# Batch 0 of a fused attention and feed-forward kernel: two pairs' kv in one PSUM bank, an earlier table load, late x blocks side by side

## The chip, the cores and the metric

One core of one Trainium2 chip. The metric is the device time of one execution in microseconds, as the median of several runs. Kernels are compared only within the same rounds. "Ratio" is always the mean time of one kernel's fast runs over that of the other's fast runs of the same rounds, so it is not quite the ratio of the medians that are quoted. A profiled span is some 1.9 us shorter than the device time of the same execution (284.4 against 286.36 for the kernel before). The experiments ran in three groups on three chips, so times are compared within a group only, and profiles by the distance between two events of one trace: the second profiles, x2 first and no late x on one; kv later and x3 on VectorE on another; the parts alone and v first on the third.

## The reference

```python
# q, k, v: 8 batches x 8 heads x 576 x 64, fp32
q_s = softmax(q, axis=head_dim)                 # per row
k_s = softmax(k, axis=sequence)                 # per column
kv  = einsum('bhsd,bhse->bhde', k_s, v)         # 64 x 64 per head
x   = einsum('bhsd,bhde->bhse', q_s, kv)        # then heads side by side: 4608 x 512
out = gelu_exact(x @ w_in) @ w_out              # w_in 512 x 2048, w_out 2048 x 512
```

## The kernel before

Everything is bf16 on TensorE with fp32 sums in PSUM. A batch goes through these stages: exp of q and k on ScalarE; normalisation and transposition of q (`qT`); `kv` of two heads at a time (a "pair", four per batch), divided by the column sums of exp(k); `x` of each pair, one 128x512 matmul, copied to SBUF as block 0 to 3 of `xT`; then h (16 tiles of 4 matmuls, one for each x block), Gelu, y. TensorE should never stand still, so each batch's attention is worked into the y matmuls of the batch before. Batch 0 has no such cover: its attention is the start of the kernel, while the weights are still arriving.

```python
def kv_pair(b, hp):                       # kv of one pair, in a bank of its own
    ps = psum_a.tile([128, 512], FP32, tag="a")
    for n in range(NS):
        nc.tensor.matmul(ps[:, 0:D + 1], ek_pair[hp // 2][:, hp % 2, n, :],
                         v_pair[b][:, hp, n, 0:D + 1], start=(n == 0), stop=(n == NS - 1))

def norm_pair(b, hp, eng1):               # column D holds the sums
    nc.vector.reciprocal(rec[:, 0:1], ps[:, D:D + 1])
    for hh in range(2):                   # second half on ScalarE if eng1 == "s"
        ...   # kvbd[...] = ps[pr, 0:D] * rec[pr, 0:1]

def x_step(b, hp, eng="v"):               # one matmul, one copy (VectorE, or ScalarE if "s")
    x_mm(b, hp); x_evac(b, hp, eng)

# batch 0 (... = cuts)
kv_pair(0, 0); tp_mm(0, 1)
norm_pair(0, 0, "v")
tp_evac(0, 1, "s")                        # second half of qT, on ScalarE
kv_pair(0, 1); norm_pair(0, 1, "v")
x_step(0, 0)
kv_pair(0, 2); kv_pair(0, 3)
x_step(0, 1, "s")
norm_pair(0, 2, "s"); norm_pair(0, 3, "s")
table(AF.Gelu)                            # a one-element Gelu, to load its table
h_phase(0, {...}, groups={0: 2},          # first two h tiles together, block by block
        pre={1: [lambda: x_step(0, 2)],   # before block 1
             2: [lambda: x_step(0, 3)]})  # before block 2
...
# batch 1, worked into the end of batch 0's y
tp_step(1, 0); tp_step(1, 1)              # after y tiles 0 to 11
...                                       # y tiles 12, 13
kv_pair(1, 0); norm_pair(1, 0, "s")       # first use of batch 1's v
y_end(0); y_end(1)                        # y tiles 14, 15 of two column blocks
...
# transfers, in the order of issue, all from one queue
# q0 k0 v0 | w_in in 5 blocks | w_out blocks 0-2 | q1 k1 | w_out block 3 (2 halves) | v1 (4 pairs) | ...
```

The softmax here doesn't subtract the row's maximum and nothing guards it: scores larger than these inputs give would overflow.

## Time and profile before

| | before |
|---|---|
| device time, median of the first 3 runs | 286.33 us (286.24 to 286.64) |
| profiled span | 284.4 us |
| TensorE busy | 97% |
| "steady h": first h tiles at full speed (weights of their last x block, block 3, loaded) | 17.68 us |
| first y matmul | 30.19 us |
| batch 1's first kv matmul | 43.17 us |
| start of the last copy of output | 281.03 us |

How to read it: the engines run beside each other, and TensorE is the one that is nearly always busy. So time can only be won where TensorE stands still. The table's middle rows are mile posts of TensorE. The prediction below shows the lines of the chain. In the profile's lines PE is TensorE, PEld its weight loads, DVE VectorE, ACT ScalarE, POOL GpSimd, and SPq and ACTq the sequencers that issue transfers; a line gives start, length, engine and what was done, and in brackets how long the engine had been idle and what ended that.

### The profile page before, as it was taken

To read this page: it belongs to the slowest core of one execution; us is meant where nothing else is said; L and a number is where in the kernel's file an instruction comes from. 1 tells how busy PE (TensorE), PEld (TensorE's weight loads), DVE (VectorE), ACT (ScalarE), POOL (GpSimd) and SP (SyncE) were. 2 spreads that over 40 slices of the span, in tenths; PEclk is the share of its full clock that TensorE was granted. 3 is DMA by queue.
4 is the path that set the end of the run, shared out by engine and by line. 5 is a ranking of instruction groups with operands and counts; after the bars stand their busy time and mean duration, and the time that the engine had idled before them with its cause. 6 is when DMAs were issued, how large, how long until landed. Compare 5 with 4: busy or idle time off the path is not lost.

```text
span 284.4 us, 3842 instructions
## 1 busy us (share of the span) xinstructions
PE 276.6 (97%) x1484; PEld 131.1 (46%) x1511; DVE 119.4 (42%) x239; ACT 159.7 (56%) x266; POOL 38.6 (14%) x34
## 2 busy tenths in 40 slices
PE   8989999999999999999999999999999999999995
PEld 3534455445445445444544454445444444444443
DVE  7664388028696454354434532453225111110012
ACT  4876595779565934694368526872576165017400
POOL 5830033002020050005000500040001300000000
PEclk9999999999999999999999999999999999999999
DMA  7999999999529939922993199517500600120033
GB/s 239 378 383 387 372 388 309 308 298 233 143 62 268 297 92 246 248 96 88 233 271 102 74 212 277 140 74 170 127 0 37 184 2 0 74 76 0 0 74 76
DMA packets 58593, 50.05 MB, mean 176 GB/s; under 512 B 26704, under 2 KB 48464, under 8 KB 58576
## 3 DMA queue, kind: packets, MB, share of 16 engines
q1 hardware_dynamic: 58288, 49.68, 61.1%
q8 instruction: 12, 0.20, 0.3%
q10 hardware_dynamic: 288, 0.13, 0.2%
q14 instruction: 5, 0.04, 0.1%
HBM read 36.70 MB, written 9.44 MB: 162 GB/s over the span
## 4 chain that ended last, share of the span: by engine, by line
PE 91%; DMA 3%; DVE 2%; ACT 2%; issue 1%; DVEq 0%; ACTq 0%
PE ps L376 40%; PE ps L386 40%; PE ps L476 3%; DMA f<-in_k_dram 3%; PE ps L251 2%; PE ps L408 1%; PE ps L346 1%; PE ps L323 1%; DVE xT L356 1%; ACT ek L145 1%; DVE kvbd L212 1%; PE ps L197 1%; PE ps L255 0%; PE ps L288 0%; ACT L145 0%
## 5 line engine op out<-in xcount | busy, mean ns | idle before, releaser
L381 ACT ACTIVATE g<-ps 128x512 bf16<-128x512 f32 x144 | 85.7, 597 | 93.4 <-PE ps L376 93.4
L376 PE MATMUL ps<-xT,wi_bf 128*128 128x512 bf16 x560 | 128.6, 379 | 1.3 <-DVE xT L356 0.3
L386 PE MATMUL ps<-wo_bf,g 128*128 128x512 bf16 x549 | 123.2, 379 | 0.6
L376 PEld LDWEIGHTS <-wi_bf 128*128 128x128 bf16 x576 | 55.3, 98 | 66.0 <-issue 2.8
L386 PEld LDWEIGHTS <-g 128*128 128x128 bf16 x560 | 54.6, 98 | 64.9
L393 DVE COPY y_sb<-ps 128x512 f32<-128x512 f32 x35 | 23.9, 686 | 74.9 <-PE ps L386 74.6
L243 POOL TENSOR_TENSOR e<-e,recq 128x1024 bf16<-128x1024 bf16 (+1 forms) x10 | 27.6, 2761 | 178.8 <-ACT ek L148 95.7
L356 DVE CAST xT<-ps 128x512 bf16<-128x512 f32 x32 | 20.6, 686 | 32.6 <-PE ps L346 22.5
L241 DVE TENSOR_REDUCE qsum<-e 128x16 f32<-128x1024 bf16 (+1 forms) x13 | 21.1, 1624 | 8.4 <-ACT e L145 7.0
L224 DVE CAST v_aug<-f 128x512 bf16<-128x512 f32 x24 | 10.3, 429 | 10.0 <-DMA f<-in_v_dram 9.3
L148 ACT ACTIVATE e<-f 128x512 bf16<-128x512 f32 (+2 forms) x28 | 13.2, 540 | 0.1
L97 ACT ACT_TABLE_LOAD x9 | 11.5, 1283 | 2.8 <-issue 2.6
L273 DVE TENSOR_SCALAR kvbd<-ps,rec 64x64 bf16<-64x64 f32 x48 | 11.6, 280 | 0.8
L476 PE MATMUL ps<-kvbd 128*128 128x512 bf16 x35 | 10.3, 462 | 1.2 <-DVE scr L85 1.2
L148 ACT ACTIVATE ek<-f 128x512 bf16<-128x512 f32 x20 | 10.9, 613 | 0.0
L182 ACT ACTIVATE ek<-f 64x1152 bf16<-64x1152 f32 x8 | 9.3, 1162 | 1.7 <-DMA f<-in_k_dram 1.5
L145 ACT ACTIVATE e<-f 128x1024 bf16<-128x1024 f32 (+1 forms) x7 | 6.8, 990 | 3.2 <-DMA f<-in_q_dram 3.2
L251 PEld LDWEIGHTS <-ek 128*128 128x128 bf16 x96 | 6.8, 97 | 3.2 <-ACT ek L145 0.6
L251 PE MATMUL ps<-v_aug,ek 128*128 128x129 bf16 x96 | 8.1, 220 | 0.1
L467 DVE CAST wo_bf<-w 128x2048 bf16<-128x2048 f32 (+1 forms) x5 | 5.1, 1014 | 5.8 <-DMA w<-in_moe_w_out_dram 5.7
L476 PEld LDWEIGHTS <-kvbd 128*128 128x128 bf16 x35 | 3.9, 116 | 6.6 <-issue 3.2
L216 DVE CAST vr_aug<-f 64x512 bf16<-64x512 f32 x6 | 2.5, 416 | 8.7 <-DMA f<-in_v_dram 8.7
(52 smaller groups left out, 98.6 us busy)
## 6 DMA issues: line engine op xcount, KB each, us to landing
out_dram<-y_sb SPq DMA_DIRECT2D x32, 256.0 KB, 2.4
f<-in_q_dram SPq DMA_DIRECT2D x6, 1024.0 KB, 7.7
f<-in_k_dram SPq DMA_DIRECT2D x6, 1024.0 KB, 10.8
f<-in_v_dram SPq DMA_DIRECT2D x6, 1024.0 KB, 9.6
w<-in_moe_w_in_dram SPq DMA_DIRECT2D x6, 512.0 KB, 8.6
w<-in_moe_w_out_dram SPq DMA_DIRECT2D x3, 1024.0 KB, 12.8
f<-in_k_dram SPq DMA_DIRECT2D x4, 576.0 KB, 8.6
f<-in_v_dram SPq DMA_DIRECT2D x8, 288.0 KB, 8.1
```

The source lines that it names most:

```text
L97: nc.scalar.activation(out=scr[:, 1:2], in_=scr[:, 0:1], func=func)
L148: nc.scalar.activation(out=dst[:, s::4], in_=src[:, u::4], func=AF.Exp)
L241: nc.vector.reduce_sum(out=qsum, in_=eq[:, :, hs, :], axis=AX.X)
L243: eng.tensor_tensor(out=eq[:, :, hs, :], in0=eq[:, :, hs, :], in1=recq.unsqueeze(3).to_broadcast([128, J, w, D]), op=ALU.mult,)
L251: nc.tensor.matmul(ps, st[b]["ek"][:, j, hs, :].rearrange("p h d -> p (h d)"), v_aug[b % 2][:, j, hp, 0:PW], start=(j == 0), stop=False,)
L273: nc.vector.tensor_scalar_mul(out=kvbd[b][pr, hps[i], c * 64:c * 64 + 64], in0=ps[pr, i, c * (D + 1):c * (D + 1) + D], scalar1=rec[pr, i:i ...
L356: nc.vector.tensor_copy(out=st[b]["xT"][:, hp, :], in_=ps)
L376: nc.tensor.matmul(ps, wi_bf[:, dm, t * 128:(t + 1) * 128], xT[:, dm, :], start=(dm == 0), stop=(dm == NDM - 1),)
L381: nc.scalar.activation(out=g[:, t, :], in_=ps, func=AF.Gelu)
L386: nc.tensor.matmul(ps, st[c]["g"][:, t, j * 128:(j + 1) * 128], wo_bf[:, t, :], start=(t == 0), stop=(t == NDF - 1),)
L393: nc.vector.tensor_copy(out=y_sb, in_=ps)
L476: nc.tensor.matmul(ps, zeros[:, 0:128], zeros, start=True, stop=True)
```

## The change

The intent is to shorten the stretch from 12 to 18 us. Pairs 2 and 3 share a PSUM bank, so that one reciprocal and two multiplies (with the reciprocal broadcast along the row) serve both. The Gelu table is loaded right after the exps. ScalarE copies x0 and x1, VectorE copies qT. x2 and x3 are both multiplied ahead of the second x block of h, and copied by two engines side by side.

```diff
+    def kv_two(b):
+        ps = psum_a.tile([128, 2, 256], FP32, tag="a")
+        ...                            # pair 2+i in ps[:, i, :], one pair after the other
+    def norm_two(b):
+        nc.vector.reciprocal(rec, ps[:, :, D])
+        for hh in range(2):
+            pr = slice(hh * 64, hh * 64 + 64)
+            nc.vector.tensor_tensor(out=kvbd[b][pr, 2:4, ...], in0=ps[pr, :, 0:D],
+                in1=rec[pr].unsqueeze(2).to_broadcast([64, 2, D]), op=ALU.mult)
@@ batch 0 @@
     tp_mm(0, 1)
+    table(AF.Gelu)
     norm_pair(0, 0, "v")
-    tp_evac(0, 1, "s")
     kv_pair(0, 1)
     norm_pair(0, 1, "v")
-    x_step(0, 0)
-    kv_pair(0, 2)
-    kv_pair(0, 3)
+    x_step(0, 0, "s")
+    tp_evac(0, 1)
+    kv_two(0)
     x_step(0, 1, "s")
-    norm_pair(0, 2, "s")
-    norm_pair(0, 3, "s")
-    table(AF.Gelu)
+    norm_two(0)
     h_phase(0, {...}, groups={0: 2}, pre={
-        1: [lambda: x_step(0, 2)],
-        2: [lambda: x_step(0, 3)],
+        1: [lambda: x_step(0, 2), lambda: x_step(0, 3, "s")],
     })
```

More of the change, by code (lines that the diff above doesn't have):

```diff
@@ L212, in norm_pair @@
                 nc.vector.tensor_scalar_mul(out=dst, in0=ps[pr, 0:D], scalar1=rec[pr, 0:1])
+    def kv_two(b):
+        ps = psum_a.tile([128, 2, 256], FP32, tag="a")
+        st[b]["kvt"] = ps
+        for i in range(2):
+            for n in range(NS):
+                nc.tensor.matmul(
+                    ps[:, i, 0:D + 1], ek_pair[1][:, i, n, :], v_pair[b][:, 2 + i, n, 0:D + 1],
+                    start=(n == 0), stop=(n == NS - 1),
+                )
+    def norm_two(b):
+        ps = st[b]["kvt"]
+        rec = small.tile([128, 2], FP32, tag="reck")
+        nc.vector.reciprocal(rec, ps[:, :, D])
+        for hh in range(2):
+            pr = slice(hh * 64, hh * 64 + 64)
+            nc.vector.tensor_tensor(
+                out=kvbd[b][pr, 2:4, hh * 64:hh * 64 + 64], in0=ps[pr, :, 0:D],
+                in1=rec[pr].unsqueeze(2).to_broadcast([64, 2, D]), op=ALU.mult,
+            )
     def cast_vr(b):
```

## The prediction

> **What bounds the kernel now.** I read the page first: shares of the engines and the chain that ended last.
>
> ```profile
> PE 276.6 (97%) x1484; PEld 131.1 (46%) x1511; DVE 119.4 (42%) x239; ACT 159.7 (56%) x266; POOL 38.6 (14%) x34
> PE 91%; DMA 3%; DVE 2%; ACT 2%; issue 1%; DVEq 0%; ACTq 0%
> ```
>
> TensorE is busy 97% of 284.4 us and carries 91% of the chain. A change that leaves the matmuls alone can win only where TensorE waits. The change touches batch 0's attention step, so next I asked for the chain of waits from 10 to 19 us:
>
> ```profile
> 14.00 0.29 DVE kvbd L212
> 14.29 0.03 issue
> 14.32 0.69 DVE xT L356
> 15.01 0.08 DVE rec L205
> ...
> 15.12 0.28 DVE kvbd L212
> 15.39 0.09 DVE rec L205
> 15.48 0.01 issue
> 15.49 0.32 ACT kvbd L210
> 15.81 0.05 issue
> 15.86 0.40 PE ps L323
> 16.26 0.02 issue
> 16.28 1.35 DVE xT L356 x2
> 17.63 0.04 issue
> 17.68 1.46 PE ps L376 x6
> ```
>
> Columns are start, length, what. Between 12.6 and 17.6 us VectorE sets the pace: copy of x0, normalisation of pair 2 (its second half on ScalarE), the x2 matmul, then two x copies one after the other. Only at 17.68 does TensorE begin the last input block of the first two h tiles; from there it runs without a gap (11.95 us busy of the stretch 18 to 30). This 5 us is all that the change can shorten.
>
> Then I asked where a shift of TensorE would meet something that does not shift. The stretches of busy time and the timelines of GpSimd and TensorE around batch 1's first kv say:
>
> ```profile
> 30.00:45.00 15.00, 14.95 (x96) 7.66 (x97) 10.68 (x15) 10.56 (x12) 4.50 (x5) 1.00 1.07 376
> 42.13 1.42 POOL L188 CAST v_aug<-f 128x576 bf16<-128x576 f32 x2 [3.35 <-DMA f<-in_v_dram]
> 41.45 1.89 PE L386 MATMUL ps<-wo_bf,g 128*128 128x512 bf16 x8
> 43.17 0.45 PE L197 MATMUL ps<-v_aug,ek 128*128 128x65 bf16 x9
> ```
>
> In the first line the last two figures are the DMA share (1.07, so full) and 376 GB/s. GpSimd sat idle 3.35 us for batch 1's v and cast its first pair from 42.13; that cast lasts 0.67 us (664 to 669 ns), so it is done at 42.80. The kv matmul that needs it started at 43.17. Batch 1's v is held by a full DMA, not by compute; TensorE is some 0.3 us behind it.
>
> **What the Trainium skill says.** (1) "VectorE: DVE Perf Modes", section on the TRN2 errata, gives an fp32 tensor_tensor as (N+151)/0.96 ns. For N=128 that is 291 ns (estimate from that page). The trace has no such shape, but its 128x1024 tensor_tensor took 1225 ns at best against 1224 by the formula, and its PSUM copy of 128 columns 292 ns. (2) "SBUF — State Buffer", Who interferes with whom, says that a VectorE instruction with at most one SBUF input outside the 2-port modes does not contend with GpSimd. The new multiplies read PSUM and one SBUF operand, so GpSimd's weight casts at 14.26 to 16.9 us should not stretch them. The trace shows the other side only: tensor_tensor with two SBUF inputs took 1600 ns at 38.26 us, where GpSimd was still busy until 38.78, against 1225 alone. (3) "ScalarE: Activation LUTs", What ACT_TABLE_LOAD costs: about 1283 ns for the load plus a 1380 ns drain. The trace agrees on the load (mean 1283 ns) but not on a drain here: load at 16.14, next activation at 17.44. (4) "PSUM — Partial Sum Buffer", The four PSUM rules: two accumulation groups open at once in one bank must not both clear it. Here pair 2's nine matmuls end before pair 3's first, so one bank is safe; no run shows it yet.
>
> **The change, part by part.** The counts come from comparing the two kernels' instruction order, which keeps TensorE's 3024 instructions in number.
>
> ScalarE, table load ahead: the last exp ends at 8.17+4.72 = 12.89. Load and dummy activation take 17.64-16.14 = 1.50 us, so ScalarE is free at about 14.4. The copy of x0 moves to it: 14.4+0.59 = 15.0. Before, VectorE ended that copy at 14.32+0.69 = 15.01. No change for the first h matmuls (15.06). x1's copy follows to 15.55, 0.2 later than before (15.36), not needed until 16.2. Before, the Gelu table was ready at 17.64 and the first Gelu waited for TensorE until 18.09, so the load's old place cost nothing directly; its real effect is to take qT's copy off ScalarE.
>
> VectorE: gets qT's second copy (0.69 us, as the 128x1024 copy at 10.72) in place of x0's copy (0.69 us): 14.30 to 14.99, nothing won. Reciprocal of both pairs: one of 160 to 169 ns in place of two of 150 to 155; starts at about 14.92 by the overlap seen at 14.93. Multiplies start 0.19 later, as before (14.93 to 15.12): two of 0.29 end at 15.10+0.29+0.29 = 15.68. Before, pair 2 was ready at 15.81 through ScalarE and pair 3 at 16.12. x2's matmul can start at 15.68+0.05 = 15.73, against 15.86: 0.13 us won.
>
> Late x: x3's matmul now follows x2's at once (0.22 later, 15.95). VectorE copies x2 from 15.73+0.42 = 16.15 to 16.84 (0.42 was the distance from 15.86 to 16.28). ScalarE copies x3 beside it, 16.37 to 16.97. Before, VectorE did both in a row and ended at 17.63. TensorE: block 1 of two tiles at 16.17 and 16.38, block 2 at 16.84+0.07 = 16.91 and 17.12, block 3 at 17.34, when x3 has been ready for 0.37. Before: 17.68. Won at the start of steady h: 17.68-17.34 = 0.34 us, of which 0.13 from the normalisation and 0.21 from copying side by side (TensorE's own two block-2 matmuls take over from the wait).
>
> Batch 1: the gain arrives at kv's matmul, which would start at 43.17-0.34 = 42.83; the cast at 42.80 plus about 0.06 (12.06 to 12.12 was that step in batch 0) allows 42.86. So about 0.31 remains, and 0.03 is lost. The other pairs' casts end at 43.55, 44.3 and 45.1, the kv matmuls would start at 44.0, 45.0, 46.1: no wait. The w_out casts at 40.00 and 41.35 end 0.7 and 1.6 us before their matmuls. After that I find no wait of TensorE for a transfer; Gelu, exp and copies follow TensorE and move with it. Sum: 0.31 us, rounded down to 0.28 for small waits not foreseen. 286.33-0.28 = 286.05 us, 0.1% faster.
>
> **The rivals.** First, v's arrival caps more: if casts or their signals are slower than read, 0.1 of the 0.31 goes; time 286.15. For it: GpSimd's 3.35 us wait and the full DMA. Second, the opposite: the freed VectorE casts wi's third block 0.7 us earlier (16.84 against 17.54), its buffer is returned earlier, the w_out load behind it is issued earlier and v lands earlier; then all 0.34 stays, or more. Against it: DMA shares of 1.03 to 1.09 in every stretch from 16 to 44 us, so an earlier issue only queues longer. Time 285.95 to 286.0. Third, the multiply with a broadcast operand is slow (0.45 each, or stretched by GpSimd): x2 starts at 16.05, block 2 at 17.23, block 3 at 17.66, and nothing is won: 286.3. Fourth, ScalarE becomes the bound: if the table load costs the page's drain as well, x0 is ready only at 16.4, x1 at 17.0, the h start slips by 0.5 to 1 us: 286.8 to 287.3. The gap of 0.02 between load and activation in the trace speaks against it.
>
> **Range and chances.** The three runs before spread from 286.24 to 286.64, so the noise is as large as the gain. The mechanism gives -0.4 to +0.1 for likely cases. Range: 285.70 to 286.40 us, prediction 286.05. 2% would be 5.7 us, more than the whole 5 us stretch of waits: faster by over 2% 0.005, slower by over 2% 0.005, within 2% 0.99.
>
> **What would show it.** Right: in the changed profile the two multiplies last about 0.29 us each; x2's and x3's copies overlap on VectorE and ScalarE; the uninterrupted h matmuls start near 17.34; batch 1's first kv matmul starts near 42.86, directly behind GpSimd's cast, which still starts near 42.13. Wrong: multiplies over 0.4 us; x0's copy ending well after 15.0; a cast of v that has moved with the change; or a new wait of TensorE after 44 us that swallows the rest.

## The result, and the profile after

The changed kernel took 286.37 us in the median (286.12 to 286.59, 6 runs), the kernel before in the same rounds 286.44 (286.04 to 287.34, 6 runs). The ratio is 0.9995, with a 95% interval of 0.998 to 1.0011: the same, and no gain that stands clear of the scatter.

The first profile of the changed kernel, though, seems to give what was promised. Its page:

```profile
PE 275.7 (97%) x1484; PEld 130.7 (46%) x1511; DVE 118.7 (42%) x237; ACT 159.0 (56%) x265; POOL 38.5 (14%) x34
PE 87%; DMA 6%; ACT 4%; issue 1%; DVE 1%; SPq 0%; ACTq 0%
```

The span is 284.2 us, and the last copy starts at 280.77, 0.26 before that of the kernel before. But the chain now has 6% DMA and 4% ScalarE where it had 3% and 2%. Between 10 and 19 us the chain of waits (start, length, what) shows why:

```profile
12.19 1.16 ACT ek L182
...
13.36 1.28 ACT L97
...
14.66 0.20 ACT scr L97
14.86 0.48 ACT xT L380
...
15.38 0.39 PE ps L398
...
15.83 0.39 PE ps L345
...
16.24 0.70 DVE xT L378
...
16.99 2.10 PE ps L398 x9
```

VectorE no longer sets the pace. In this execution batch 0's k came 0.45 us later than in the profile before (exps end at 13.35, not 12.89), and the early table load now stands between the exps and x0's copy: x0 is ready at 15.34, where the prediction had 15.0. VectorE had normalised pairs 2 and 3 by 15.27 (two multiplies, 0.59 us together from 14.68) and then waited.

The timelines of GpSimd and TensorE at batch 1's first kv, the same kernel:

```profile
41.93 2.94 POOL L188 CAST v_aug<-f 128x576 bf16<-128x576 f32 x4 [3.36 <-DMA f<-in_v_dram]
42.92 0.45 PE L197 MATMUL ps<-v_aug,ek 128*128 128x65 bf16 x9
```

Here v itself came 0.20 us earlier than before (41.93 against 42.13), so TensorE did not have to wait. Two things that the change does not touch, k and v, had thus moved by about as much as the gain. One profile of each kernel can't tell a gain of 0.26 us from luck, and this is what the experiments are about.

### The profile page after: what moved, and what is told of

Same layout as the page of the kernel before. It is cut to its first block, busy times and chain, and to the rows that moved or that the text cites. A ratio compares the mean times of both kernels' runs of the same rounds, so it can differ in the third digit from the quotient of the medians.

```text
span 284.2 us, 3838 instructions
## 1 busy us (share of the span) xinstructions
PE 275.7 (97%) x1484; PEld 130.7 (46%) x1511; DVE 118.7 (42%) x237; ACT 159.0 (56%) x265; POOL 38.5 (14%) x34
## 4 chain that ended last, share of the span: by engine, by line
PE 87%; DMA 6%; ACT 4%; issue 1%; DVE 1%; SPq 0%; ACTq 0%
PE ps L398 40%; PE ps L408 40%; DMA f<-in_k_dram 6%; PE ps L273 2%; ACT ek L182 2%; PE ps L430 1%; PE ps L368 1%; PE ps L345 1%; ACT ek L145 1%; PE ps L277 0%; ACT L145 0%; ACT L97 0%; PE ps L197 0%; ACT e L145 0%; SPq L108 0%
## 5 line engine op out<-in xcount | busy, mean ns | idle before, releaser
L378 DVE CAST xT<-ps 128x512 bf16<-128x512 f32 x30 | 19.2, 685 | 33.0 <-PE ps L368 22.5
L498 PE MATMUL ps<-kvbd 128*128 128x512 bf16 x35 | 9.2, 424 | 1.2 <-DVE scr L85 1.2
```

Of the source, the lines that this page charges most:

```text
L378: nc.vector.tensor_copy(out=st[b]["xT"][:, hp, :], in_=ps)
L498: nc.tensor.matmul(ps, zeros[:, 0:128], zeros, start=True, stop=True)
```

## The experiments

The theory after the result: the front of the kernel does gain some 0.3 us, but batch 1's v decides how much of it is kept, and v's arrival scatters from one execution to the next. Rivals: the front gains nothing (the 0.26 us is scatter); or v moves with the change.

### The two kernels again

No edit; a control, and a second profile of each.

> The kernel before, unchanged, as a control. Theory A (the change's gain of about 0.26 us in the profiles is real and only smaller than the scatter of the times): ratio to before 1.000 with a scatter of single times of 0.3 us or more; steady h begins within 0.1 us of 17.68, batch 1's first kv matmul within 0.1 us of 43.17. Theory B (the 0.26 us is scatter of the arrival of transfers at the start): steady h of this second profile of the same code begins 0.2 us or more away from 17.68.

Measured: 286.68 us against 286.68, ratio 1.000 (0.9988 to 1.0013), single runs 286.25 to 286.98. The timelines of GpSimd and TensorE:

```profile
42.50 1.44 POOL L188 CAST v_aug<-f 128x576 bf16<-128x576 f32 x2 [3.35 <-DMA f<-in_v_dram]
43.22 0.45 PE L197 MATMUL ps<-v_aug,ek 128*128 128x65 bf16 x9
```

Steady h began at 17.56, 0.12 us earlier than in the first profile (theory A allowed 0.1), yet the kv matmul came 0.05 later. v was cast from 42.50, 0.37 later, and the matmul followed 0.72 behind: the cast's 0.67 and a signal. So the kernel before waits for v too, in some executions, and the 0.3 us of slack that the prediction read was that of one execution.

> The changed kernel, unchanged, a second profile. Theory A: steady h begins at 17.3 to 17.45 again, last copy of the output 0.2 to 0.35 us earlier than in the control's profile; ratio 0.9985 to 1.0. Theory B: steady h anywhere from 17.3 to 17.8, following the arrival of k and of the first w_in block.

Measured: 286.86 us, ratio 1.0007 (0.9995 to 1.002), span 285.0.

```profile
43.01 1.43 POOL L188 CAST v_aug<-f 128x576 bf16<-128x576 f32 x2 [3.35 <-DMA f<-in_v_dram]
43.72 0.45 PE L197 MATMUL ps<-v_aug,ek 128*128 128x65 bf16 x9 [0.21 <-POOL v_aug L188]
20.40 9.40 PEld L398 LDWEIGHTS <-wi_bf 128*128 128x128 bf16 x45 [0.48 <-DVE wi_bf L478]
```

The same code, and v is a full 1.08 us later than in its first profile; the last copy starts at 281.57, 0.80 later. The third line shows a second such place: h of batch 0 waits at 20.4 us for the last part of w_in's third block. Block 3 of h had begun at about 17.44 (block 2's weights at 17.01, two matmuls of 0.216 later), as expected; but what came of it at the end was the opposite of what was expected of the end. Steady h held; the last copy and the ratio missed.

### x2 ahead of the first h pair

```diff
-        1: [lambda: x_step(0, 2), lambda: x_step(0, 3, "s")],
+        0: [lambda: x_step(0, 2)],
+        1: [lambda: x_step(0, 3, "s")],
```

> The changed kernel with x2's matmul ahead of the first pair's h instead of the second's, x3's left ahead of the second. In the changed kernel's profile VectorE idled 0.97 us before x2's copy, because x2's matmul stood behind the first h block, which waited for x0 and for w_in's cast. If that order is what holds the end of the stage, x2 is copied from about 15.7, block 2 goes on without a wait, and steady h begins at about 17.05, 0.35 earlier than the changed kernel. Then batch 1's first kv matmul meets the cast of v: of 0.6 us gained against before, about 0.3 to 0.45 stays. If the order doesn't matter, steady h stays at 17.4.

Measured: 286.48 us, ratio 0.9995 (0.9981 to 1.0009). A miss. VectorE's 0.97 us of waiting in the changed kernel's first profile was a matter of that execution, in which kv began early (first reciprocal at 12.17) and k late. Here VectorE's multiplies ended at 15.65, x2's matmul followed at 15.71, and x3, now behind two h matmuls, was copied only from 16.79. First y came 17.43 us after the first reciprocal, no better than the changed kernel (17.28 where no transfer disturbs it, below). v gated again (cast 42.45, kv 43.16).

### Without the late x: how much does v let through?

Wrong result (relative error 0.37): x2 and x3 are dropped, h of batch 0 reads blocks 0 and 1 twice, so TensorE is about 1 us ahead.

```diff
-        1: [lambda: x_step(0, 2), lambda: x_step(0, 3, "s")],
-                        ps, wi_bf[:, dm, t * 128:(t + 1) * 128], xT[:, dm, :],
+                        ps, wi_bf[:, dm, t * 128:(t + 1) * 128], xT[:, dm % 2 if c == 0 else dm, :],
```

> Wrong result on purpose: batch 0's h reads x0 and x1 twice, x2's and x3's matmuls and copies are gone. Tests the cap by batch 1's v. Steady h begins at about 16.7 to 16.8, which with the two matmuls dropped (0.43 us) puts TensorE about 1 us ahead of before. Theory cap: batch 1's first kv matmul starts directly (0.06 us) behind the cast of v, near 42.8 to 43.0, TensorE shows a wait there of 0.4 to 0.7 us, and only 0.2 to 0.45 us of the 1 us reaches the end. Rival, v moves with the change: cast of v 0.5 us or more earlier than the control's, no wait, 0.9 to 1.0 us at the end (ratio 0.9966).

Measured: 286.29 us, ratio 0.9996 (0.9981 to 1.001). In its profile (GpSimd, TensorE, and VectorE's last copy):

```profile
42.05 2.18 POOL L188 CAST v_aug<-f 128x576 bf16<-128x576 f32 x3 [3.35 <-DMA f<-in_v_dram]
42.76 0.45 PE L197 MATMUL ps<-v_aug,ek 128*128 128x65 bf16 x9 [0.22 <-POOL v_aug L188]
280.62 0.29 DVE L435 COPY y_sb<-ps 128x128 f32<-128x128 f32 x1 [0.34 <-PE ps L430]
```

The first y matmul started at 29.12, 1.07 us ahead of before. At 42.76 only 0.41 of it was left, and 0.41 reached the end (281.03 to 280.62). v had not come earlier in return: its cast began 0.08 from that of the first profile. An advance of a whole microsecond is cut by v, as the theory had it, and more than half of it was lost; the rival is out.

### Batch 1's first kv later among the y matmuls

To take v out of the way, the last y matmuls were regrouped so that the first kv stands 0.43 us later while every kv keeps the same work ahead of its x. Three kernels: on before, on after, on the one without late x.

```diff
-    kv_pair(1, 0); norm_pair(1, 0, "s")
     y_end(0)
+    kv_pair(1, 0); norm_pair(1, 0, "s")
     y_end(1); y_out(0, yps[0], 0)
     kv_pair(1, 1); norm_pair(1, 1, "s")
-    x_step(1, 0)
     y_end(2)
+    x_step(1, 0)
```

> The kernel before, with batch 1's kv matmuls regrouped: two of batch 0's last y matmuls go ahead of the first kv, and two others move from before x0 to between kv 1 and x0, so every kv keeps the same work between itself and its x. In six profiles the last copy of the output started 237.85 us after batch 1's first kv matmul, and that matmul never started earlier than 0.71 us after the start of the cast of v; the start of that cast scattered from 41.93 to 43.01. Theory (arrival of v sets the end): the first kv now needs v 0.43 us later, so it waits rarely; last copy at steady h + 263.3, near 281.0, in nearly all executions, scatter smaller, ratio to before 0.999 to 0.9997. Rival (v doesn't matter, the scatter comes from elsewhere): ratio 1.000, same scatter.

Measured: 286.82 us, ratio 1.0013 (1.0 to 1.0027): slower, if anything. A miss of my own making, which the profile shows at x1's matmul:

```profile
46.00 0.39 PE L323 MATMUL ps<-qT,kvbd 128*128 128x512 bf16 x1 [0.31 <-ACT kvbd L210]
```

I had counted TensorE's work between each kv and its x, but not VectorE's order: the copy of a y block (0.67 us) now stands right between the normalisations of pairs 0 and 1. The wait of 0.31 us for it is the price. The single runs did draw together, though: 286.64 to 287.07.

> The changed kernel with the same regrouping. Theory: with v out of the way the changed front shows: 0.15 to 0.3 us better than the regrouped kernel before, last copy of the output at 280.7 to 280.85, ratio to before 0.998 to 0.999. Rival (the front of the change gains nothing): equal to the regrouped kernel before.

Measured: 286.55 us, ratio 1.000 (0.9985 to 1.0015). With the same price in both, the pair can be compared in the profiles: last copy at 280.97 against 281.29, so 0.32 us. First y is 17.29 us after VectorE's first reciprocal, against 17.59: 0.30 for the change. The first reciprocal was 0.07 earlier as well, which is not the change's doing, and 0.05 was lost at v (kv 13.46 us after the first y, against 13.41). The expected size of 0.15 to 0.3 was met by the front and passed by a hair at the end. The expected last copy (280.7 to 280.85) and ratio (0.998 to 0.999) were missed, which the price of 0.31 us can account for.

> Wrong result on purpose, as the run without late x, with the regrouping: TensorE is about 1 us ahead of before at the start of y. Theory: v gates again, at 0.43 us less: last copy at (start of the cast of v) + 0.71 + 237.42 or a few tenths later if the last w_out cast gates, near 280.3; 0.3 to 0.5 us better than the ungrouped one at equal arrival of v.

Measured: 286.09 us, ratio 0.9994 (0.9975 to 1.0014); in the profiled execution 287.07, with the last copy at 281.72. A miss. That execution's transfers were late from the start: h waited 0.72 us for the last part of w_in's third block (cast at 20.13), so TensorE's advance was gone before y began (30.34), and v's cast started at 43.19. It says that v is not the only gate: w_in's third block is another, 23 us earlier.

### x3 copied by VectorE

The part "side by side", undone alone.

```diff
-        1: [lambda: x_step(0, 2), lambda: x_step(0, 3, "s")],
+        1: [lambda: x_step(0, 2), lambda: x_step(0, 3)],
```

> The changed kernel with x3 copied by VectorE behind x2 instead of by ScalarE beside it. The term of copying side by side was put at 0.21 us: the two copies then follow each other on VectorE (1.35 us), block 3 starts about 1.40 us after the start of x2's copy instead of about 1.18, so steady h begins 0.2 us later relative to VectorE's first reciprocal (from +4.8 to +5.0 us). At the end nothing of it need show: the first kv waits for v anyway in most executions, ratio to before 0.9995 to 1.001.

Measured: 286.53 us, ratio 1.0002 (0.9983 to 1.0022), single runs from 285.87 to 287.44. VectorE's timeline:

```profile
16.51 1.29 DVE L378 CAST xT<-ps 128x512 bf16<-128x512 f32 x2 [0.48 <-PE ps L345]
```

Both copies end at 17.80, 4.88 us after the first reciprocal (12.92), and block 3's first matmul follows at 17.85, or +4.93. In the changed kernel undisturbed it begins at +4.76 (below). Copying side by side is worth 0.17 us at that place; 0.21 was predicted, 0.2 expected here. At the end nothing shows: this execution's v came latest of all, 43.54.

### v's first pair ahead of w_out's last half

The experiment that should free the end: the transfer of v's first pair is issued 512 KB earlier, and w_out's last half comes and is cast in two quarters.

```diff
-    wo.append(load_wo(3, 2))
-    load_pair(1, "v", v, 4)
+    # w_out block 3: first half; v pair 0; third quarter; fourth quarter; v pairs 1, 2, 3
@@ batch 1 @@
-    cast_wo(3, wo[3], 2, 2)
     tp_step(1, 0)
+    cast_wo(3, wo[3], 2, 1)
+    cast_wo(3, wo[3], 3, 1)
     tp_step(1, 1)
```

> The changed kernel with the transfer of batch 1's first v pair issued ahead of the second half of w_out's last block, which is loaded and cast in two quarters. Theory (v's arrival sets the end): in ten profiles so far the cast of v began 21.72 us (21.70 to 21.74) after the first cast of w_in's fourth block and gated the first kv in six of the eight that have the kernel's own order; now it begins about 1.34 us (512 KB at 385 GB/s) earlier, about 20.4 us after that cast, and never gates. The first kv then starts 12.98 us after the first y matmul, the last copy of the output at about 280.8, and the ratio to before is 0.998 to 0.999. Rival (the lateness only moves to w_out's last quarters, which land 0.75 us later): a wait of TensorE at the y matmuls behind the first kv, ratio 0.9995 to 1.0005.

Measured: 286.52 us, ratio 1.0005 (0.9988 to 1.0021), single runs from 286.0 to 287.36. The profiled execution is the shortest of the correct ones, a span of 284.1. VectorE, ScalarE and the weight loads at the front, then GpSimd, VectorE, TensorE and the last copy:

```profile
14.98 0.59 DVE L231 TENSOR_TENSOR kvbd<-ps,rec 64x128 bf16<-64x128 f32 x2
16.06 0.69 DVE L378 CAST xT<-ps 128x512 bf16<-128x512 f32 x1 [0.48 <-PE ps L345]
16.27 0.58 ACT L380 CAST xT<-ps 128x512 bf16<-128x512 f32 x1 [0.71 <-PE ps L345]
16.80 1.17 PEld L398 LDWEIGHTS <-wi_bf 128*128 128x128 bf16 x6 [0.41 <-issue]
40.65 0.66 POOL L188 CAST v_aug<-vf 128x576 bf16<-128x576 f32 x1 [2.00 <-DMA vf<-in_v_dram]
41.98 0.43 DVE L489 CAST wo_bf<-w 128x512 bf16<-128x512 f32 x1 [0.20 <-DMA w<-in_moe_w_out_dram]
42.32 0.69 DVE L319 COPY qT<-ps 128x1024 bf16<-128x1024 bf16 x1
42.73 0.45 PE L197 MATMUL ps<-v_aug,ek 128*128 128x65 bf16 x9
43.21 0.17 DVE L205 RECIPROCAL rec<-ps 128x1 f32<-128x1 f32 x1 [0.21 <-PE ps L197]
280.58 0.29 DVE L435 COPY y_sb<-ps 128x128 f32<-128x128 f32 x1 [0.34 <-PE ps L430]
```

This is the front as it was predicted. The two multiplies take 0.59 us, the copies of x2 and x3 overlap, the weights of blocks 2 and 3 are loaded in one run from 16.80, so block 3 begins at 16.80+0.43 = 17.23, 4.76 us after the first reciprocal at 12.47. v is cast 20.37 us after w_in's fourth block instead of 21.72, and kv follows y by 12.98 us with no wait. But the times as a whole are no better. The expected ratio of 0.998 to 0.999 was missed, and 1.0005 is what the rival expected; which executions were slow and why is not known, as only the first has a trace.

This trace does keep the rival open. VectorE waited 0.20 us for w_out's last quarter, cast it 21.70 us after w_in's fourth block, and had behind that cast, in its own order, qT's copy (until 43.00) and the reciprocal of the first kv (43.21). So a stream of transfers only 0.2 to 0.3 us later, measured from the first reciprocal, would have held up this reciprocal and the normalisation behind it. An estimate from the table below: here w_in's fourth block was cast 7.81 us after the first reciprocal, so the limit lies near 8.1, and 8 of the 14 executions are beyond it; in the kernel's own order 10 of them wait for v (worked out further down). The edit took v out of the way, but another transfer of the same late stream stands right behind it.

> The same two edits on the kernel before. Theory: no wait for v; last copy of the output 0.15 to 0.35 us later than in the changed kernel with v first, near 281.05 (steady h + 263.4), ratio to before 0.9990 to 0.9997. If the change's front were worth nothing, the two kernels with v first would have the same steady h against VectorE's first reciprocal and the same end.

Measured: 286.16 us, ratio 0.999 (0.9977 to 1.0003), runs from 286.07 to 286.39. In the profile there is no wait for v (cast 41.15, kv 42.91; VectorE's reciprocal behind it came 0.05 us late, just behind qT's copy), last copy at 280.76. Against its counterpart that is 0.18 us later. The times point the other way (286.16 against 286.52), with intervals that overlap. First y 17.60 us after the first reciprocal, against 17.28 with the change: 0.32 us for the front, again; the first reciprocal itself, 12.33 against 12.47, took 0.14 of it back.

### Two parts alone, on the kernel before

```diff
+    kv_two(0)          # for kv_pair(0, 2), kv_pair(0, 3)
+    norm_two(0)        # for norm_pair(0, 2, "s"), norm_pair(0, 3, "s")
```

> The kernel before with only pairs 2 and 3 in one bank, one reciprocal and two broadcast multiplies. Relative to VectorE's first reciprocal the kernel before has x2's matmul at +3.25, block 3 of h at +5.08. Step of the prediction: 0.13 us from the normalisation. Expected: multiplies of 0.29 us each from +2.51, x2's matmul at +3.16, block 3 at +4.95 to +5.0. Rival (broadcast multiply slowed by GpSimd's casts): +5.1 or more. At the end nothing clear of scatter.

Measured: 286.57 us, ratio 1.0004 (0.999 to 1.0018). The multiplies stood where expected (+2.51 us, 0.59 together, ready at +3.10, against +3.20 for pair 2 through ScalarE in the kernel before). x2's matmul missed its +3.16 and came at +3.48, because the h matmuls ahead of it waited:

```profile
14.40 1.17 POOL L474 CAST wi_bf<-w 128x512 bf16<-128x512 f32 x2 [0.84 <-DMA w<-in_moe_w_in_dram]
15.07 0.61 PE L398 MATMUL ps<-xT,wi_bf 128*128 128x512 bf16 x2 [0.80 <-POOL wi_bf L474]
```

In this execution kv was early (first reciprocal at 12.03), w_in's first block was not, and the gain of 0.1 us had nowhere to go. Inconclusive for block 3, but it shows a third gate.

```diff
     tp_mm(0, 1)
+    table(AF.Gelu)
...
     norm_pair(0, 3, "s")
-    table(AF.Gelu)
```

> The kernel before with only the Gelu table loaded right after the exps. ScalarE still has qT's second half, x1 and half of the normalisation of pairs 2 and 3 to do, now 1.5 us later: qT's copy ends near +2.8 after VectorE's first reciprocal, x1's at +3.4, pair 2's half at +3.75, so x2's matmul is at about +3.8 instead of +3.25 and block 3 at +5.6: 0.5 us slower front; at the end 0.2 to 0.6 us later where v does not gate (ratio 1.000 to 1.002). If the place of the load doesn't matter (the prediction's words: it cost nothing where it was), block 3 stays at +5.1.

Measured: 286.93 us, ratio 1.0015 (1.0002 to 1.0028), last copy at 281.60 with no wait for v. The order of events was as expected, the size was not. ScalarE and TensorE:

```profile
14.56 0.99 ACT L299 COPY qT<-ps 128x1024 bf16<-128x1024 bf16 x1
15.45 0.59 ACT L358 CAST xT<-ps 128x512 bf16<-128x512 f32 x1
16.07 0.51 ACT L210 ACTIVATE kvbd<-ps,rec 64x64 bf16<-64x64 f32 x2
16.43 0.39 PE L323 MATMUL ps<-qT,kvbd 128*128 128x512 bf16 x1 [0.33 <-ACT kvbd L210]
```

x2's matmul came at +3.38 instead of +3.25 (first reciprocal 13.05), first y at +17.71 instead of +17.59: 0.12 us slower, not 0.5. Most of the 1.5 us went into ScalarE's idle times (in the profile before 0.16 us ahead of qT's copy, 0.71 ahead of x1's, 0.13 ahead of pair 2's half). So the load's place did cost something with ScalarE's work of the front behind it, and this part should help only together with the others, which move that work to VectorE. Of the 0.57 us by which the last copy is later than in the first profile, 0.44 is the later first reciprocal and 0.12 the front; the ratio, some 0.4 us, is more than the front explains.

### All profiles side by side

Starts in us from the traces; "1st rec" is VectorE's first reciprocal of kv, "4th w_in" VectorE's first cast of w_in's fourth block, "v cast" GpSimd's first of batch 1.

| kernel | 1st rec | first y | y after rec | 4th w_in | v cast | first kv | kv after v cast | last copy |
|---|---|---|---|---|---|---|---|---|
| before | 12.61 | 30.19 | 17.58 | 20.41 | 42.13 | 43.17 | 1.04 | 281.03 |
| before, again | 12.48 | 30.08 | 17.60 | 20.80 | 42.50 | 43.22 | 0.72 | 281.07 |
| after | 12.17 | 29.94 | 17.77 | 20.22 | 41.93 | 42.92 | 0.99 | 280.77 |
| after, again | 12.68 | 30.12 | 17.44 | 21.27 | 43.01 | 43.72 | 0.71 | 281.57 |
| x2 first | 12.54 | 29.97 | 17.43 | 20.71 | 42.45 | 43.16 | 0.71 | 281.01 |
| no late x | 12.92 | 29.12 | 16.20 | 20.34 | 42.05 | 42.76 | 0.71 | 280.62 |
| x3 on VectorE | 12.92 | 30.66 | 17.74 | 21.80 | 43.54 | 44.26 | 0.72 | 282.11 |
| two alone | 12.03 | 29.83 | 17.80 | 20.61 | 42.33 | 43.04 | 0.71 | 280.89 |
| table alone | 13.05 | 30.76 | 17.71 | 20.57 | 42.32 | 43.74 | 1.42 | 281.60 |
| before, v first | 12.33 | 29.93 | 17.60 | 20.79 | 41.15 | 42.91 | 1.76 | 280.76 |
| after, v first | 12.47 | 29.75 | 17.28 | 20.28 | 40.65 | 42.73 | 2.08 | 280.58 |
| before, kv later | 12.52 | 30.11 | 17.59 | 20.38 | 42.10 | 43.52 | 1.42 | 281.29 |
| after, kv later | 12.45 | 29.74 | 17.29 | 20.72 | 42.43 | 43.20 | 0.77 | 280.97 |
| no late x, kv later | 12.68 | 30.34 | 17.66 | 21.48 | 43.19 | 43.96 | 0.77 | 281.72 |

Three things are rigid. The last copy starts 237.85 us (237.85 to 237.86) after the first kv, in all eleven profiles with that kv in its own place. The v cast starts 21.70 to 21.75 us after w_in's fourth block, in all but the two that move v's transfer (20.36 and 20.37). And the first kv follows y by 12.98 us or v's cast by 0.71, whichever is later, again in all eleven (give or take 0.01). So, for a kernel with that kv in its place, the end of an execution is known from two numbers at 20 and 30 us: how far TensorE is, and how late the stream of transfers is.

## Why the prediction was right or wrong

**The time.** 286.37 lies in the range, and "within 2%" was right. That says little for the prediction: the range also held no gain at all (286.33, the median that the prediction started from), and 286.37 is 0.03 from its upper end. The point, 286.05, was 0.3 us too low, and the predicted gain of 0.28 us is not what was measured: 0.07 between the medians, 0.14 by the ratio with an interval from 0.6 faster to 0.3 slower.

**The front.** Shown, and well sized. Where no transfer disturbs it, block 3 of h begins 4.76 us after the first reciprocal instead of 5.08, and the first y 17.28 or 17.29 instead of 17.59 or 17.60: 0.30 to 0.32 us where 0.34 was predicted. Of its terms, the multiplies of 0.29 us were right (0.59 for two), and so was the absence of a contest with GpSimd: the second multiply took 294 ns in the kernel without late x, where GpSimd's cast had ended 0.02 us after its start, and 295 ns wholly beside a cast (v first), just as "SBUF — State Buffer", Who interferes with whom, has it for a multiply with one operand in SBUF. Copying side by side gave 0.17 at its place instead of 0.21; the normalisation alone gave 0.10 in its own reading instead of 0.13. The shared PSUM bank, of which the prediction could show nothing, gave correct results.

**"Batch 1: ... about 0.31 remains, and 0.03 is lost."** This is the step that failed. Its mechanism, v held by the full DMA and the kv matmul behind the cast, is shown by the experiment without late x, which lost 0.66 of 1.07 us there. Its size was read from a single trace in which v happened to be early. v's cast scatters from 41.93 to 43.54 over the profiles with the kernel's own order of transfers, five times the slack of 0.31. An estimate from the table: take each of the 14 executions' first reciprocal and w_in time, and let the first kv be the later of (reciprocal + 17.59 + 12.98) and (w_in + 21.72 + 0.71) for before, with 17.28 in place of 17.59 for after. The kernel before then waits for v in 8 of 14, the changed one in 10; the change keeps all of its 0.31 us in 4, part of it in 2, nothing in 8, and 0.115 us on average. That lies inside the intervals of both comparisons of the same two kernels (ratios 0.9995 and 1.0007), which are too wide to prove it or to tell it from no gain.

**The rivals.** The first (v caps more) is the one that came true, in a stronger form than the 0.1 us given to it. The second (v moves with the change) is out: 21.72 us after w_in's fourth block before and after. The third (slow multiply) is out. The fourth (ScalarE becomes the bound) was dismissed because of the missing drain, and the drain is indeed missing, but it came true in another way in one execution: where k was late (exps until 13.35) and kv early (first reciprocal at 12.17), exps, table load and x0's copy were the longest path of the front, and first y stood at +17.77. The prediction took the exps' end from one trace as fixed, just as it did with v.

**"After that I find no wait of TensorE for a transfer."** Right: from the first kv to the end every kernel with that kv in its place takes the same 237.85 us. But before it there are gates that the one trace did not show: w_in's first block (0.80 us in one execution) and its third (0.48 and 0.72).

**What stays open.** Why the stream of transfers is up to 1.6 us later at w_in's fourth block in one execution than in another (20.22 to 21.80). It is not the amount moved, or not that alone: summed over 0 to 20 us by the rates of five stretches, the kernel with x3 on VectorE (21.80) had moved 6.65 MB and the kernel before (20.41) 6.60; two other late ones (21.27 and 21.48) had moved 6.51, which at some 380 GB/s is 0.2 to 0.4 us of their lateness. The landings narrow it down. The parts of w_in come at an even pace, 0.65 to 0.70 us for each quarter of the third block and 1.34 to 1.37 for each half of the blocks after it, except for one jump: from the third quarter of the third block to the first half of the fourth it takes 2.02 us in the first profile of the changed kernel, which is the even pace, and up to 3.57 in that with x3 on VectorE. In all 14 profiles one packet of another kind, which the profile calls "instruction", runs just before: 16 KB in 1.04 to 1.12 us, starting between 17.26 and 17.97 us, the only one of its size in the first 30 us. In the first profile of the kernel before, the view of DMA queues from 17.2 to 17.4 us (packets, MB, share of 16 engines) has it:

```profile
q8 instruction: 1, 0.02, 32.9%
```

The jump adds 0 to 0.6 us in the five executions where this packet took 1.04 or 1.05 us, and 0.6 to 1.5 in the nine where it took 1.09 or more. That it causes the jump is a guess, not shown: no run moves it, and the records do not part the sixteen DMA engines, so whether it holds up one of them can't be told. A better version is not proven either: the change with v first gave the shortest profile of a correct kernel but no better times, and the ratio of 0.999 of the kernel before with v first has an interval that includes 1.

## What to carry to other kernels

Before a gain of tenths of a microsecond is promised, look for the next place downstream where the path meets a full DMA queue, and take several traces of the unchanged kernel: the slack at that place is a distribution, and a gain is kept only in the executions where it is positive. Measure such a change as a difference between two events of the same trace (here, first y after first reciprocal: 17.59 against 17.28), which showed it where total times with a scatter of a microsecond could not. And when work is regrouped on one engine, check the order it forces on the others: 0.31 us went to a copy that came to stand between two normalisations.

## What the Trainium skill lacked or had wrong

- "ScalarE: Activation LUTs", What ACT_TABLE_LOAD costs: it adds a drain of about 1380 ns to every switch. Here the next activation started 1.30 us after the start of a load of 1.28 (13.36 to 14.66 in the changed kernel; 13.16 to 14.45 with the table alone), so no drain shows between a load and the activation that follows, nor ahead of the load (last exp until 13.35, load from 13.36).
- "VectorE: DVE Perf Modes", the section on the TRN2 errata: its tensor_tensor formula is checked there for 512 and 2048 elements; it also held for 128 elements on 64 partitions with one operand from PSUM and the other a broadcast column (282 to 295 ns, 291 by the formula).
- No page read for this case gives the scatter of a transfer's landing from one execution to the next: 20.22 to 21.80 us for the same block at equal bytes moved, and then a stream so even that v, 21.7 us later, landed within 0.04 us of its place in it (21.68 to 21.72 us behind that block).
